# Windowed attention and an MLP mixer on one core: q and k of ten head pairs transposed by DMA instead of by TensorE

## The chip, the cores and the metric

One core of one Trainium2 chip runs the kernel. The metric is the device time of one execution, in microseconds. Three executions of the kernel before took 206.72, 207.12 and 207.36 us; the median is 207.12. A fourth execution ran under the hardware profiler, and every duration below is from it.

## What is computed

Attention with a window of 128 keys and 4 sink keys (batch 4, 8 heads, 768 positions, head size 64), and then a mixer on its output (model width 512): a small MLP over positions, added to its input, and an MLP over channels, added again. The inputs are float32; the kernel works in bf16 with float32 accumulation.

```python
scores = scale * np.matmul(q, k.transpose(0, 1, 3, 2))
is_sink = pos[None, :] < 4
rel = pos[:, None] - pos[None, :]
keep = is_sink | ((rel >= 0) & (rel < 128))
a = softmax(np.where(keep, scores, -1e9))
x = concat_heads(np.matmul(a, v))                        # 4 x 768 x 512
h = np.maximum(x.transpose(0, 2, 1) @ w_tok1, 0.0) @ w_tok2   # 768 -> 256 -> 768
u = x + h.transpose(0, 2, 1)
out = u + np.maximum(u @ w_ch1, 0.0) @ w_ch2             # 512 -> 1536 -> 512
```

## The kernel before

**The unit of attention is a pair of heads.** There are 16 pairs, p = 0 to 15, four for each batch element. A pair's q and k are held as bf16 tiles q_bf and k_bf, 128 partitions x (6 rows, 2 heads, 64 columns). Scores need the head dimension on the partitions, so both are transposed into qT and kT (128 x 768: 64 columns of each of the two heads by 768 positions). Scores are matmuls of kT and qT into PSUM, ACT takes the exponential into pT, DVE masks it, and matmuls of pT with v_aug (v with a column of ones) give values and sums, which DVE turns into x_sb.

**Loads.** Pairs 0 to 3 come as float32 over SP's queue. Pairs 4 to 15 are loaded and cast by POOL's queue, one DMA for each head of q and of k (96 KB in bf16, 'half' below; `load_cast`, line 104), one DMA for v (192 KB, `load_v`). Six pairs of q_bf and k_bf are kept (NQ, line 54); the load of pair p waits until pair p - 6 has been transposed (line 984). The weights, w_ch1 and w_ch2 in four quarters each, go through the same queue between the pairs (lines 1025 to 1040): w_ch2's quarters come behind pairs 4 to 7. In `rows_of` (line 85) a partition holds six consecutive rows of q, which lie together in HBM (1536 bytes).

**Transposing.** For pairs 5 to 15, `transposed` (line 447) gives PE 24 transposes of 64 rows (12 of q, 12 of k; line 455) into one of the two score banks in PSUM. ACT or DVE copy qT and kT out (lines 129 and 131), undoing the order of the rows, and DVE then clears a part of the bank (`cleared`, line 470). Pair 4 and the first four are transposed by `turn` (line 429) in other banks. qT has 2 buffers, kT has 4 (NKB).

**Order.** The program is written by a planner, class `Plan`, that holds a cost and dependences for each piece of work (`Op`) and a clock for each engine, and issues instructions in the order that these give; each engine then runs its own instructions in that fixed order. PE's work comes in three lists: the first batch element's attention; `main`, the channel MLP of all four (`mix_channels`: v1 units with w_ch1, out_part units with w_ch2); and `side`, the attention and token mixing of the other three (`attention_and_tokens`, line 846). How main and side are interleaved is a written list, MERGED: "9/25" puts side unit 9 once 25 main units have been placed. Work with 64 rows is grouped in bursts, since PE loses time in changing between 64 and 128 rows. The burst that scores pair p begins with the transposes of pair p + 1 (lines 855 to 863).

**The end of the work.** out_part sums twelve matmuls in a PSUM bank, DVE adds u (line 924) into one of three o_sb buffers, and SP issues the store (line 930).

Of the kernel before, what the change touches and what calls it, by code (L numbers as in the profile page):

```python
# [10 lines left out]
BF16 = mybir.dt.bfloat16  # L11
# [5 lines left out]
def kernel(  # L17
# [13 lines left out]
    nc = tc.nc  # L31
    B, H, S, D = q.shape
    P = 128
    NT = S // P
# [10 lines left out]


    MERGED = (
        "1/0 0/2 2/4 3/8 4/15 5/17 6/17 7/19 8/24 9/25 10/25 11/27 12/27 13/29 14/29 15/30 16/32 17/32 18/35 "
        "19/36 20/38 21/38 22/38 23/41 25/42 26/42 24/42 27/44 28/48 29/50 31/52 30/52 32/56 33/57 34/57 "
        "35/60 36/61 39/63 40/63 41/65 42/67 38/67 37/67 43/71 44/76 45/76 46/76 47/80 50/82 48/82 49/82 "  # L50
        "51/86 52/92 53/95 54/95 55/95 56/100 57/102 58/102 59/105 60/106 62/115 67/115 63/115 61/118 64/120 "
        "65/121 66/128 68/130 69/131 70/133 71/135 72/135 73/135 74/138"
    )
    NQ = 6
    NPT = 3
    MASKED_BY_PE = [(p, g) for p in range(NHP) for g in range(NT // 2) if (p, g) != (NHP - 1, 0)]

    singles = ctx.enter_context(tc.tile_pool(name="singles", bufs=1))
    qkv_pool = ctx.enter_context(tc.tile_pool(name="qkv", bufs=NQ))
    raw_pool = ctx.enter_context(tc.tile_pool(name="raw", bufs=4))  # L60
    att_pool = ctx.enter_context(tc.tile_pool(name="att", bufs=2))
    pt_pool = ctx.enter_context(tc.tile_pool(name="pt", bufs=NPT))
    mix_pool = ctx.enter_context(tc.tile_pool(name="mix", bufs=2))
    v1_pool = ctx.enter_context(tc.tile_pool(name="v1", bufs=1))
# [16 lines left out]
    in_order = tc.keep_in_program_order  # L81
# [3 lines left out]
    def rows_of(pidx, n):  # L85

        b, hp = pairs[pidx]
        return (q, k)[n][b, 2 * hp:2 * hp + 2].rearrange("h (p j) d -> p h j d", j=NT)

    def load_raw(pidx):  # L90
        raw = []
# [6 lines left out]
    bfs = {}  # L98
# [28 lines left out]
    def copy(e, out, in_):  # L127
        if e == "ACT":
            in_order(nc.scalar.activation(out, in_, AF.Copy))  # L129
        else:  # L130
            in_order({"DVE": nc.vector, "POOL": nc.gpsimd}[e].tensor_copy(out=out, in_=in_))  # L131
# [10 lines left out]
    done = {}  # L142
    tiles = {}
# [7 lines left out]
    def keep_warm(n, slot):  # L151
# [18 lines left out]
        out=ident, in_=ident, compare_op=ALU.not_equal, fill=1.0, base=0, pattern=[[-1, P]], channel_multiplier=1,  # L170
    ))
    in_order(nc.gpsimd.affine_select(
        out=mask_add[:, :, 0], in_=mask_add[:, :, 0], compare_op=ALU.is_ge,
# [3 lines left out]
        out=mask_add[:, :, 1], in_=mask_add[:, :, 1], compare_op=ALU.is_ge,  # L177
# [6 lines left out]
    NKB = 4  # L184
    kTb = [singles.tile([P, S], BF16, name=f"kT{n}") for n in range(NKB)]
# [8 lines left out]
    for n in range(4):  # L194
# [3 lines left out]
            out=v_sink_f[rows, odd::2, i, 0:D],  # L198
            in_=v[0].rearrange("(p o i) s d -> i o s p d", i=2, o=2)[i, odd, 0:n_sink],
# [186 lines left out]
    def piece(ns, fn, deps, need, then, keys=()):  # L386
        op = Op({}, fn, deps, then, size=float(ns))
        op.need, op.keys = need, keys
        return op

    QH = NT // 2

    def prepare(p):

        kT = kTb[p % NKB]
        parts = 2 if p <= NHP else 1

        def evict(e, n, part):
            name = ("q", "k")[n]
            if n:  # L400
                t = kT
            elif ("qT", p) in tiles:
                t = tiles["qT", p]
            else:
                t = tiles["qT", p] = att_pool.tile([P, S], BF16, name="qT2")
            to = t.rearrange("d (x p j) -> d x p j", x=2, j=NT)
            copy(e, to if parts == 1 else to[:, part], tiles["ps_" + name, p] if parts == 1 else tiles["ps_" + name, p][part])

        free = ([("sk", p - 2)] if p >= 2 else [], [(n, p - NKB) for n in ("s", "sk")] if p >= NKB else [])
        if parts == 2:  # L410
            cost = {"DVE": 540.0, "ACT": 500.0}
        else:
            cost = {"DVE": 950.0} if p < NHP else {"DVE": 950.0, "ACT": 900.0}
        for n, name in enumerate(("qT", "kT")):
            done[name, p] = [
                Op(dict(cost), lambda e, n=n, part=part: evict(e, n, part), free[n]) for part in range(parts)
            ]
            for part, op in enumerate(done[name, p]):
                op.urgent = (3 - part) * (p < NHP)
        tiles["kT", p] = kT  # L420
# [26 lines left out]
    def transposed(p):  # L447

        def run():
            ps = turned_bank(p)  # L450
            for n in range(2):
                for j in range(NT):
                    for x in range(2):
                        rows = ds(D * x, D)
                        in_order(nc.tensor.transpose(ps[:, x, n, j], bfs[p, n][rows, j], ident[rows, rows]))  # L455
                tiles["ps_" + "qk"[n], p] = ps[:, :, n].rearrange("d x j p -> d x p j")

        then = [*done["qT", p], *done["kT", p]]
        then.append(cleared(p, then))
        return piece(  # L460
            350, run, [done["q_bf", p], done["k_bf", p]], {"sc": [then]}, then, [("tq", p), ("tk", p)],
        )

    def turned_bank(key):

        tiles["ps_turned", key] = bank("sc")
        t = tiles["ps_turned", key].bitcast(BF16).rearrange("d x n b c -> d x n (b c)")[:, :, :, 2 * D:8 * D]
        return t.rearrange("d x n (j p) -> d x n j p", j=NT)

    def cleared(key, readers):  # L470

        op = Op(
            {"DVE": 400.0}, lambda e: in_order(nc.vector.memset(tiles["ps_turned", key][0:D, :, :, 3], 0.0)), readers,
        )
        op.urgent = 2
        return op

    def width(g):
        return 3 * P if g == NT // 2 - 1 else 4 * P
# [19 lines left out]
    def scores(p, g):  # L499
# [49 lines left out]
        x = done["exp", p, g] if by_pe else Op({}, None)  # L549
        x.cost, x.fn, x.deps = {"ACT": 190.0 + 1.5 * width(g)}, exp, [("pv", p - NPT)] if p >= NPT else []  # L550
        x.urgent = 2 * (p < NHP)
# [9 lines left out]
    def score_sinks(p):  # L561
# [17 lines left out]

        x = Op({"ACT": 580.0}, exp, [("pv", p - NPT)] if p >= NPT else [])  # L580
        for n in (p - 1, p):
# [94 lines left out]
    def sink_rows(p):  # L676
        def both(e):
            for i in range(2):
                r = D * i + ODD * (p % 2)
                copy(e, v_sinks[p % NHP][r:r + n_sink, i], vs[p][0:n_sink, i, 0])  # L680

        done["vs", p] = Op({"ACT": 440.0, "DVE": 400.0}, both, [done["v", p], done["pv", p - NHP]])
        return done["vs", p]
# [138 lines left out]
    def first_attention():  # L822
# [5 lines left out]
        for p in range(NHP):  # L828
            for g in range(NT // 2):
                if (p, g) in MASKED_BY_PE:  # L830
                    masks.append(masked(p, g))
# [14 lines left out]
    def attention_and_tokens():  # L846

        parts, units = [], []
        first, last = NHP, len(pairs) - 1
        prepare(first)  # L850
        units += [turn(first, n) for n in range(2)]
        for p in range(first, last + 1):
            b, hp = pairs[p]
            pieces = []
            if p < last:
                prepare(p + 1)
                pieces.append(transposed(p + 1))
            pieces.append(scores(p, 0))
            if p > first:
                pieces.append(sink_values(p - 1))  # L860
            if p == last:
                pieces.append(turned_u(b, 0, "sc"))
            units.append(burst(*pieces))
            if p > first:
                units += [values(p - 1, i) for i in range(2)]
            pieces = [scores(p, 1), scores(p, 2)]
            if hp == 0 and p > first:
                units.append(mix_h(b - 1, 1, 0, NTOK))
                units += [mix_u(b - 1, 1, st, 2) for st in range(0, NT, 2)]
                pieces.append(turned_u(b - 1, 1))  # L870
            if hp == NHP - 1 and p < last:
                pieces.append(turned_u(b, 0))
            if hp % 2 == 0:
                pieces.append(score_sinks(p + 1))
            units.append(burst(*pieces))
            units[-1].then.append(sink_rows(p))
            if hp == 2:
                units.append(mix_h(b, 0, 0, NTOK))
                units += [mix_u(b, 0, st, 2) for st in range(0, NT, 2)]
            if hp == 0 and p > first:  # L880
                parts.append(units)
                units = []
        units += [pv(p, half) for half in range(2)]
        units.append(mix_h(b, 1, 0, NTOK))
        units += [mix_u(b, 1, st, 2) for st in range(0, NT, 2)]
        units.append(burst(turned_u(b, 1)))
        return parts + [units]
# [108 lines left out]
    plan = Plan()  # L996
# [98 lines left out]
```

## Time and profile before

| | |
|---|---|
| median of three runs | 207.12 us |
| profiled execution | 206.41 us |
| its span, first to last instruction | 204.6 us |
| PE busy | 197.6 us, 97% |
| ACT, DVE busy | 113.8 us, 112.4 us |
| share of PE in the chain that ended last | 85% |
| DMA queue of POOL | 11.80 MB in 67,232 packets |
| DMA queue of SP | 9.45 MB in 5,968 packets |
| DMAs of q_bf, k_bf from issue to landing, median | 6.8 us, 5.9 us |

The span is the time from the first to the last instruction that the profiler recorded; 1.8 us of the execution lie around it. Engines are PE (TensorE matmuls), PEld (its weight loads), DVE, ACT, POOL and SP. A row of the order of time gives start, duration, engine, line, operation, the tile written and the tiles read, and how many instructions were put together. A matmul's end is modelled, so two that follow each other overlap in these rows. The instruction order of a program, with the semaphores that an instruction waits for, is known for both kernels from their builds; durations are known for the kernel before alone.

### The profile page before, as it was taken

The numbers are of one execution on the slowest core, as the hardware profiler recorded it, in microseconds if no ns is written. First come the engines' busy times: TensorE is split into PE (matmuls) and PEld (weight loads), VectorE is DVE, ScalarE is ACT, GpSimd is POOL, SyncE is SP. The second block draws the span as 40 slices with busy tenths as digits, with TensorE's granted clock in tenths as the row PEclk, the third lists the DMA queues.
The fourth block names the chain that finished last, engine by engine and source line by source line (L and its number), as shares of the span: only waits on it lengthen the run. The fifth ranks groups of instructions, "written<-read, shape, count | busy, mean of one in ns | idle before, by whom it ended". The sixth has DMA issues, their size and how long they took to land.

```text
span 204.6 us, 5496 instructions
## 1 busy us (share of the span) xinstructions
PE 197.6 (97%) x2377; PEld 119.3 (58%) x2377; DVE 112.4 (55%) x238; ACT 113.8 (56%) x195; POOL 67.3 (33%) x86
## 2 busy tenths in 40 slices
PE   6798999999999999999999999999999999999994
PEld 2345985566665665667656545666655645665453
DVE  4775653657788766866948557572654361001222
ACT  4898668879706535886563145886750114773000
POOL 6299859795699891450000000000000000000000
DMA  6999999999999999193001112100002112000223
GB/s 193 292 257 188 169 177 191 160 172 206 157 180 189 187 184 198 22 128 20 3 0 54 53 64 97 51 5 0 0 3 103 51 54 103 0 3 0 103 103 103
DMA packets 73223, 21.58 MB, mean 105 GB/s; under 512 B 63216, under 2 KB 70256, under 8 KB 73200
## 3 DMA queue, kind: packets, MB, share of 16 engines
q0 software_dynamic: 67232, 11.80, 73.1%
q1 hardware_dynamic: 5968, 9.45, 13.1%
q8 instruction: 18, 0.29, 0.6%
q14 instruction: 5, 0.04, 0.1%
HBM read 26.75 MB, written 6.29 MB: 161 GB/s over the span
## 4 chain that ended last, share of the span: by engine, by line
PE 85%; DMA 6%; DVE 3%; ACT 2%; POOL 1%; issue 1%; SPq 0%; POOLq 0%; ACTq 0%
PE ps_mx L122 77%; PE ps_sc L122 4%; DMA w_tok<-in_moe_w_tok_dram 4%; DMA v_sink_f<-in_v_dram 2%; PE ps_sc L455 2%; POOL v_aug L115 1%; DVE kT L131 1%; PE ps_mx L427 1%; ACT pT L539 1%; ACT qT L129 1%; PE ps_mx L125 1%; SPq L197 0%; ACT uT L129 0%; DVE u_sb L751 0%; DVE x_sb L650 0%
## 5 line engine op out<-in xcount | busy, mean ns | idle before, releaser
L122 PE MATMUL ps_mx<-uT,w_ch 128*128 128x384 bf16 x384 | 67.1, 326 | 0.1
L122 PE MATMUL ps_mx<-w_ch,v1T 128*128 128x512 bf16 (+2 forms) x312 | 66.9, 363 | 0.0
L539 ACT ACTIVATE pT<-ps_sc 128x1024 bf16<-128x1024 f32 (+1 forms) x48 | 44.4, 952 | 13.0 <-PE ps_sc L122 12.9
L122 PEld LDWEIGHTS <-w_ch 128*128 128x128 bf16 x384 | 36.0, 98 | 23.9 <-issue 1.2
L135 ACT ACTIVATE v1T<-ps_mx 128x384 bf16<-128x384 f32 x77 | 37.7, 490 | 19.5 <-PE ps_mx L122 18.9
L122 PEld LDWEIGHTS <-v1T 128*128 128x128 bf16 x312 | 28.3, 98 | 27.6 <-issue 0.5
L924 DVE TENSOR_TENSOR o_sb<-ps_mx,u_sb 128x512 f32<-128x512 f32 x23 | 15.8, 687 | 34.6 <-PE ps_mx L122 34.6
L122 PEld LDWEIGHTS <-w_tok 128*128 128x128 bf16 x192 | 18.3, 98 | 5.9 <-DMA w_tok<-in_moe_w_tok_dram 0.7
L107 POOL DMA_DIRECT2D q_bf<-in_q_dram x24 | 19.6, 822 | 4.4 <-DMA w_ch<-in_moe_w_ch_dram 2.2
L107 POOL DMA_DIRECT2D k_bf<-in_k_dram x24 | 19.6, 820 | 4.1 <-DMA w_ch<-in_moe_w_ch_dram 1.7
L751 DVE TENSOR_TENSOR u_sb<-ps_mx,x_sb 128x512 bf16<-128x512 f32 x20 | 13.2, 687 | 13.0 <-PE ps_mx L122 12.9
L115 POOL DMA_DIRECT2D v_aug<-in_v_dram x16 | 16.4, 1026 | 8.3 <-ACT v_sink L129 7.1
L131 DVE COPY kT<-ps_sc 128x768 bf16<-128x768 bf16 x11 | 10.5, 958 | 13.4 <-ACT qT L129 13.4
L122 PEld LDWEIGHTS <-pT 128*128 128x128 bf16 x352 | 14.1, 98 | 3.3 <-issue 0.6
L129 ACT ACTIVATE qT<-ps_sc 128x768 bf16<-128x768 bf16 x11 | 8.9, 810 | 12.3 <-PE ps_sc L455 12.1
L122 PE MATMUL ps_mx<-v_aug,pT 128*128 128x65 bf16 x352 | 15.6, 194 | 0.0
L547 DVE TENSOR_TENSOR pT<-pT,mask_main 128x1024 bf16<-128x1024 bf16 (+1 forms) x24 | 14.3, 619 | 1.3 <-ACT pT L539 1.3
L122 PE MATMUL ps_sc<-qT,kT 64*64 64x192 bf16 (+3 forms) x288 | 14.4, 248 | 0.0
L135 ACT ACTIVATE h1T<-ps_mx 128x512 bf16<-128x512 f32 (+1 forms) x8 | 4.1, 517 | 17.1 <-PE ps_mx L122 16.9
L122 PE MATMUL ps_mx<-h1T,w_tok 128*128 128x256 bf16 x96 | 13.2, 273 | 0.0
L137 DVE TENSOR_SCALAR v1T<-ps_mx 128x384 bf16<-128x384 f32 x19 | 10.4, 549 | 4.9 <-PE ps_mx L122 4.9
L122 PE MATMUL ps_mx<-x_sb,w_tok 128*128 128x256 bf16 x96 | 12.0, 273 | 0.5 <-DMA w_tok<-in_moe_w_tok_dram 0.4
(68 smaller groups left out, 156.6 us busy)
## 6 DMA issues: line engine op xcount, KB each, us to landing
out_dram<-o_sb SPq DMA_DIRECT2D x23, 256.0 KB, 2.0
v_aug<-in_v_dram POOLq DMA_DIRECT2D x16, 192.0 KB, 7.2
w_ch<-in_moe_w_ch_dram POOLq DMA_DIRECT2D x8, 384.0 KB, 8.8
q_bf<-in_q_dram POOLq DMA_DIRECT2D x24, 96.0 KB, 6.8
k_bf<-in_k_dram POOLq DMA_DIRECT2D x24, 96.0 KB, 5.9
q_f<-in_q_dram SPq DMA_DIRECT2D x4, 384.0 KB, 5.0
k_f<-in_k_dram SPq DMA_DIRECT2D x4, 384.0 KB, 5.7
w_tok<-in_moe_w_tok_dram POOLq DMA_DIRECT2D x2, 384.0 KB, 7.7
```

The lines of the kernel that those rows point to most:

```text
L107: in_order(nc.gpsimd.dma_start(out=out[:, h], in_=rows[:, h]))
L115: in_order(nc.gpsimd.dma_start(out=v_aug.rearrange("p i t d -> p (i t) d")[:, :, 0:D], in_=v[b].rearrange("h s d -> (h s) d")[2 * hp * S:2 ...
L122: in_order(nc.tensor.matmul(*args, skip_group_check=True, **kwargs))
L129: in_order(nc.scalar.activation(out, in_, AF.Copy))
L131: in_order({"DVE": nc.vector, "POOL": nc.gpsimd}[e].tensor_copy(out=out, in_=in_))
L135: in_order(nc.scalar.activation(out, in_, AF.Relu))
L137: in_order(nc.vector.tensor_scalar_max(out=out, in0=in_, scalar1=0.0))
L455: in_order(nc.tensor.transpose(ps[:, x, n, j], bfs[p, n][rows, j], ident[rows, rows]))
L539: in_order(nc.scalar.activation(part(tiles["pT", p][:, :, ds(2 * g, 2)]), of_keys(tiles["ps_s", p, g])[:, :, 0:width(g)], AF.Exp, scale=scale,
L547: in_order(nc.vector.tensor_tensor(out=pt, in0=pt, in1=m, op=ALU.mult))
L751: in_order(nc.vector.tensor_tensor(out=u_part(b, g, s0, n), in0=tiles["ps_u", b, g, s0], in1=x_sb[b][:, s0:s0 + n, c0:c0 + cn], op=ALU.add,))
L924: in_order(nc.vector.tensor_tensor(out=o_sb.rearrange("p (g c) -> p g c", g=2), in1=u_rows(b, st), in0=tiles["ps_out", b, st].rearrange("p ...
```

## The change

From pair 6 on (BY_DMA), q_bf and k_bf are loaded with row p of each of the six 128-row tiles on partition p, and `prepare` no longer makes transposes and copies. It plans two operations on SP instead, a DMA each, which read the bf16 tile in SBUF and write qT or kT in SBUF transposed. They wait for the loads and for the buffers that they write (4 of qT now, 4 of kT). The burst of pair p no longer holds the transposes of pair p + 1 when p + 1 is 6 or more; the score bank, the copies and the clearing that belonged to them are gone. A load of pair p + 6 now waits for pair p's transfers. MERGED is another list. The output stores share SP's queue with the transfers. The planner's costs for a transfer are 1700 ns on SP and 2500 ns until it has landed.

```diff
     MERGED = (
-        "1/0 0/2 2/4 3/8 4/15 5/17 6/17 7/19 8/24 9/25 10/25 11/27 12/27 13/29 14/29 15/30 16/32 17/32 18/35 "
...
+        "1/0 0/2 2/4 3/8 4/16 5/16 6/17 7/17 8/21 9/23 10/25 11/25 12/27 13/29 15/29 14/30 16/32 17/32 18/32 "
...
     NPT = 3
+    BY_DMA = 6
...
-    att_pool = ctx.enter_context(tc.tile_pool(name="att", bufs=2))
+    att_pool = ctx.enter_context(tc.tile_pool(name="att", bufs=4))
...
-        return (q, k)[n][b, 2 * hp:2 * hp + 2].rearrange("h (p j) d -> p h j d", j=NT)
+        return (q, k)[n][b, 2 * hp:2 * hp + 2].rearrange(
+            "h (j p) d -> p h j d" if pidx >= BY_DMA else "h (p j) d -> p h j d", j=NT,
+        )
...
+    def turned_by_dma(p):
+
+        free = ([("sk", p - 4)], [(n, p - NKB) for n in ("s", "sk")])
+
+        def transfer(n):
+            if n:
+                t = tiles["kT", p] = kTb[p % NKB]
+            else:
+                t = tiles["qT", p] = att_pool.tile([P, S], BF16, name="qT2")
+            in_order(nc.sync.dma_start(
+                out=t.rearrange("c (j p) -> c j p", j=NT), in_=bfs[p, n].rearrange("p j h d -> p (j h d)"), transpose=True,
+            ))
+
+        for n, name in enumerate("qk"):
+            op = Op({"SP": 1700.0}, lambda e, n=n: transfer(n), [done[name + "_bf", p], *free[n]], lag=2500.0)
+            done[name + "T", p] = [op]
+            done["t" + name, p] = op
+            plan.pending.append(op)
+
     def prepare(p):
+        if p >= BY_DMA:
+            return turned_by_dma(p)
...
                 prepare(p + 1)
-                pieces.append(transposed(p + 1))
+                if p + 1 < BY_DMA:
+                    pieces.append(transposed(p + 1))
```

## The prediction

> **What bounds the kernel now.** I read the page's busy times first, then the busy table by stage, then the order of time inside one burst, then the DMA issues.
>
> ```profile
> span 204.6 us, 5496 instructions
> ...
> PE 197.6 (97%) x2377; PEld 119.3 (58%) x2377; DVE 112.4 (55%) x238; ACT 113.8 (56%) x195; POOL 67.3 (33%) x86
> ...
> DMA  6999999999999999193001112100002112000223
> ```
>
> PE has 97% of the span, DVE and ACT half of it. The DMA row (40 slices of 5.1 us) is full until 82 us and almost empty afterwards.
>
> ```profile
> core 0: us, PE busy (x) PEld busy (x) DVE busy (x) ACT busy (x) POOL busy (x), PEclk, DMA share, GB/s
> 30.00:40.00 10.00, 10.00 (x123) 5.71 (x122) 5.81 (x12) 8.19 (x16) 7.87 (x10) 1.00 1.99 174
> 40.00:50.00 10.00, 10.00 (x124) 6.31 (x123) 6.20 (x14) 8.36 (x16) 8.47 (x11) 1.00 1.68 185
> 50.00:60.00 10.00, 10.00 (x128) 6.25 (x126) 7.56 (x15) 5.04 (x9) 7.45 (x10) 1.00 2.22 162
> 60.00:70.00 10.00, 10.00 (x209) 6.05 (x208) 7.65 (x18) 6.39 (x9) 10.00 (x13) 1.00 2.15 198
> ```
>
> PE is busy for all of 30 to 70 us at a granted clock of 1.00, and the later rows say the same up to 200 us, but for 0.15 us. So the time is PE's list of work, and an edit is worth what it takes from that list, less the waits it adds. The DMA share stands near 2: the engines are shared by overlapping packets, and in this stretch a new transfer has no idle engine to go to.
>
> ```profile
> 86.33 0.33 PE L122 MATMUL ps_mx<-uT,w_ch 128*128 128x384 bf16 x1
> ...
> 86.59 0.35 PE L455 MATMUL ps_sc<-ident,q_bf 64*128 64x64 bf16 x12
> ...
> 86.78 0.34 PE L455 MATMUL ps_sc<-ident,k_bf 64*128 64x64 bf16 x12
> ...
> 86.95 0.38 PE L122 MATMUL ps_sc<-qT,kT 64*128 64x256 bf16 x4
> ```
>
> This is one burst. A matmul's row ends late because it is pipelined, so its price is the distance from its start to the next start. The 24 transposes begin at 86.59 and the scores at 86.95: **0.36 us a pair** (the chain of waits books 0.46, the last one's tail included). The changeover from 128 to 64 rows, about 0.1 us ahead of 86.59, belongs to the burst, which stays.
>
> **The change, part by part.**
>
> 1. Gone from PE: the transposes of ten pairs, 10 x 0.36 = **3.6 us**, all on the bounding engine. The two programs' instruction order agrees: 2377 matmuls become 2137, which is 10 x 24 fewer, and the 74 changes between 64-row and 128-row work stay 74.
>
> 2. Gone from ACT and DVE: per pair a copy of qT (810 ns, L129), of kT (958 ns, L131) and a clearing (272 ns, L473). Both engines have idle time (5.87 and 6.17 of 10 us in 100 to 110), so most is worth nothing. Twice PE waits for what a copy delays: at 70.56 for x_sb (L650), which DVE begins only after kT's copy of 68.39 to 69.35, and at 98.75 for an eviction behind kT's copy and the clearing. Against the usual distance of such matmuls I read 0.21 and 0.23 us lost there. I take **0.4 us**; nothing is the other bound.
>
> 3. Added on SP: 20 transfers of 192 KB. The trace has no transposing transfer. Nearest rows:
>
> ```profile
> out_dram<-o_sb SPq DMA_DIRECT2D x23, 256.0 KB, 2.0
> v_aug<-in_v_dram POOLq DMA_DIRECT2D x16, 192.0 KB, 7.2
> ```
>
> A 256 KB store from SP lands in 2.0 us, and in 4.0 to 5.1 us while loads run (its largest values, at 76 and 80 us). I take 5 us for the second transfer of a pair to land after its issue, and 1.7 us between the two issues, the planner's own number in the diff (a store's issue on SP takes 0.33). For the burst it must land in time. I laid the changed program's PE order out with the distances that before shows, and set each pair's first wait against the landing of its second k half in before. Pair 6: needed at 47.9, landed 40.05. Pair 7: 52.2 and 43.9. Pair 8: 63.8 and 55.3. Pair 9: 74.8 and 59.1. Pair 10: 84.7 and 64.0; later pairs have 19 us or more. With q issued when it lands (38.7 for pair 6), k 1.7 behind or when it lands, and 5 us, pair 6 is ready at 45.4: 2.5 us to spare, and pairs 7 and 8 have 3 us. So the latency is covered by the lead of one pair that the new order leaves; past 2.5 us more, each microsecond is paid once (a late pair pushes all behind it back too). Stores wait behind the transfers on SP: the first one behind pair 8's k, which landed at 55.3 against a store at 57.86, and three o_sb buffers stand behind that. I cost this at nothing.
>
> 4. Added on the 16 DMA engines, where I see the real price. Loads of POOL's queue land one behind another: q and k halves 0.63 us apart, v 1.51 us apart. A transfer in between holds up all loads behind it. The first four (pairs 6 and 7) run between 39 and 49 us, with the last quarters of w_ch2 queued behind them.
>
> ```profile
> 40.65 3.01 POOL L140 DMA_DIRECT2D w_ch<-in_moe_w_ch_dram  x4
> ...
> w_ch<-in_moe_w_ch_dram POOLq DMA_DIRECT2D x1, 384.0 KB, 8.7
> ```
>
> The third quarter is issued at 42.14 and takes 8.67 us: it lands at 50.81. In the changed order PE asks for it at 53.06 (53.28 before). **Cover: 2.25 us**; the fourth has 2.4. Price of a transfer: a store moves its 256 KB in about 0.7 us (two stores at 153 to 157 us make 0.52 MB in two short peaks near 390 GB/s), so 192 KB take **0.53 us**; four make 2.1. The upper bound is a v load, of the same 192 KB in 1536 small packets: 1.51. Nothing speaks for a gain; the lower bound is 0, if transfers inside SBUF fit between packets that wait for HBM. I take the store, the only row of SP's queue.
>
> 5. The loads of pairs 6 to 15 keep 768 packets of 128 B a half, but a partition's six rows no longer lie together in HBM. v's loads have that layout, and cost 1.51 / 1536 x 768 = 0.755 for as many packets against 0.63: 0.12 us more a half, eight halves ahead of w_ch2: **1.0 us**. Bounds 0 and 1.0; I take 1.0.
>
> Parts 4 and 5 make the third quarter late by 2.1 + 1.0 - 2.25 = **0.8 us** (0 to 4.8), and PE waits for it once. Past that the queue is later still, but pairs 9 to 15 have 15 us or more.
>
> 6. The merge: the same work with as many changeovers. What it moves is priced by the waits it meets, and in before PE's waits of all kinds past 30 us, changeovers aside, come to about 1 us. I cost it at 0, with 1 us either way.
>
> Sum: 206.41 (profiled execution; its span is 204.6 and 1.8 lies around it) - 3.6 - 0.4 + 0.8 = **203.2**. The median, 207.12, stands 0.7 above that execution, so I forecast **203.9**; its own range is 203.0 to 205.5.
>
> The Trainium skill has two figures for part 4 that contradict each other. "DMA: Bandwidth & Descriptors", section "Latency and other measured facts", gives 261 GB/s for a DMA transpose; an estimate from it is 0.75 us a transfer, and the sum of 203.2 would be 204.2. "VectorE: DVE Perf Modes", section "The three transpose paths", gives 1309 ns for a 128x128 transpose by DMA against 390 ns on TensorE, and advises TensorE where PSUM will do; six blocks in a row would be 7.9 us. No run here shows either yet; the 0.36 us for a whole pair of q and k on PE is far below its 390 ns a block, so I don't carry that table's DMA figure into the sum.
>
> **The rivals.**
>
> A. *Nothing is late.* Transfers between SBUF rows slip between load packets and the new layout is free: 206.41 - 4.0 = 202.4, or 203.1 by the median. For it: the store does overlap with loads. Against it: landings do spread by about 0.7 us for each store between 58 and 75 us.
>
> B. *The transposing transfer costs the engines as much as a v load*, because it is cut small. One place, the third quarter of w_ch2: 4 x 1.51 + 1.0 - 2.25 = 4.8 us late, so 206.41 - 4.0 + 4.8 = 207.2, by the median 207.9, slower than before. It decides from (4.0 + 2.25 - 1.0) / 4 = 1.3 us a transfer. For it: every small-packet row here (128 B) costs at least 1.26 us for 192 KB. Against it: SBUF to SBUF needs no HBM. At 2.5 us a transfer it is near 212.
>
> C. *SP's queue does one transfer after another, each as long as a v load takes to land* (7.2 us). A pair then takes 14.4 us against PE's pace of (132.9 - 47.9) / 9 = 9.4, and PE waits for each: 38.7 + 10 x 14.4 + 68 us of work behind pair 15's wait = 251. It decides from 4.7 us a transfer. Against it: stores issued 2.6 us apart (153.81 and 156.40) land in 2.0 each, and planner costs that can be compared lie at their rows (950 for kT's copy of 958). The second page's rule, by its figure, would be of this kind: an estimate of 264 us.
>
> D. *The written merge loses what the transposes gave*, by 2 to 3.5 us of small waits: 205.5 to 207.5. Against it: the 74 equal changeovers.
>
> That the change doesn't do what it says is excluded by the instruction order: 240 transposes gone, 20 transfers there.
>
> **How the numbers follow.** Forecast 0.42, A 0.20, B 0.22, C 0.10, D 0.06. A measurement of this kernel tells 0.3% (0.6 us) from no change. Faster: forecast, A and a third of D, 0.64. Same (206.5 to 207.7): a quarter of B and half of D, 0.08. Slower: the rest of B and D, and C, 0.28. The range holds the forecast, A, D and rather more than half of B, 0.8 together: 202.7 to 209.0; C stays outside.
>
> **What would show it.** Right: no L455 row past pair 5; the PE row of w_ch,v1T near 53 us waiting under 1.5 us for w_ch; q and k halves about 0.75 us apart; transfers landing 3 to 5 us after issue. Wrong: PE waits on a transfer at the scores of pairs 6 to 8 (latency), w_ch2 later than 54 us (B), or a wait at every pair (C).

## The result, and the profile after

The kernel after takes **212.88 us**, the median of four runs (210.87 to 214.24), against 207.03 for four runs of the kernel before (206.72 to 207.36): a ratio of 1.025 [1.020, 1.030]. It is slower, where 203.9 was forecast and 209.0 was the upper end of the range. The profiled execution, 214.24, counts as a slow one, over 1.5% above the fastest of its four, and the ratio leaves it out, but its mean clock of 0.984 is like that of the other three (0.982 to 0.984). Its span of 212.5 stands against 204.6, and the 7.9 between the two spans are looked for below.

The page of the kernel after, from its busy times, its slices and its DMA queues:

```profile
span 212.5 us, 5003 instructions
...
PE 194.7 (92%) x2117; PEld 117.5 (55%) x2137; DVE 101.5 (48%) x218; ACT 107.8 (51%) x185; POOL 67.9 (32%) x86
...
PEclk9999999999967999999999999999999999999999
DMA  6999999999999999999999511200001212000222
...
q1 hardware_dynamic: 21968, 13.38, 29.7%
```

PE works 2.9 us less than before, DVE 10.9 and ACT 6.0 less, so the work did go; PE now stands still for 17.8 us of the span instead of 7.0. Two slices, from 58 to 69 us, have a granted clock of 0.6 and 0.7, which before has nowhere. The DMA row is full until 117 us instead of 82. SP's queue has 21,968 packets instead of 5,968: 16,000 for 20 transfers, 800 each (768 of 256 bytes and 32 of 4, by the trace's packet records).

The busy table by stage of after, the stretches that the prediction showed of before:

```profile
core 0: us, PE busy (x) PEld busy (x) DVE busy (x) ACT busy (x) POOL busy (x), PEclk, DMA share, GB/s
30.00:40.00 10.00, 9.83 (x125) 5.57 (x123) 5.81 (x12) 8.22 (x16) 6.79 (x9) 1.00 1.98 174
40.00:50.00 10.00, 8.95 (x95) 5.43 (x92) 5.83 (x12) 8.04 (x16) 7.44 (x10) 1.00 2.02 136
50.00:60.00 10.00, 4.57 (x66) 2.96 (x67) 4.08 (x10) 3.73 (x5) 3.49 (x4) 0.99 1.29 177
60.00:70.00 10.00, 8.26 (x38) 4.47 (x40) 1.72 (x3) 1.20 (x2) 8.04 (x10) 0.66 2.22 154
```

Past 22 us PE stands still for 9.6 us in all (0.3 before), and 8.2 of them lie between 40 and 70 us. The order of time says why; first SP, then PE, with the idle time ahead of an instruction and what ended it in brackets:

```profile
40.17 1.32 SPq L405 DMA_TRANSPOSE qT<-q_bf  x1
41.67 1.89 SPq L405 DMA_TRANSPOSE kT<-k_bf  x1
44.13 1.62 SPq L405 DMA_TRANSPOSE qT<-q_bf  x1
46.33 4.87 SPq L405 DMA_TRANSPOSE kT<-k_bf  x1
```

```profile
51.38 0.39 PE L125 MATMUL ps_sc<-qT,kT 64*128 64x256 bf16 x4 [2.43 <-DMA kT<-k_bf]
...
61.69 0.61 PE L125 MATMUL ps_mx<-qT,kT 64*32 64x512 bf16 x2 [5.68 <-DMA kT<-k_bf]
62.23 2.74 PE L125 MATMUL ps_mx<-w_ch,v1T 128*128 128x512 bf16 x6
```

Pair 6's kT is issued at 41.67 and lets PE go at 51.4: 9.7 us. Pair 7's is issued at 46.33, SP itself is held by it for 4.87 us, and PE gets on at 61.7: 15.3 us. By the packet records the four transfers pass one after another, in 3.5, 4.5, 5.6 and 5.2 us, so pair 7's kT stands in line until 55.9. The chain that ended last goes through that one transfer:

```profile
46.33 15.31 DMA kT<-k_bf
```

After the second wait the matmuls of w_ch and v1T are 427 ns apart until 64.8, where at the full clock they are 216 apart, and those of x_sb 213 instead of 109. The table by stage has the clock in its third column from the right, 1.00 being full:

```profile
61.69:66.00 4.31, 4.31 (x14) 1.91 (x15) 0.00 (x0) 0.60 (x1) 4.04 (x5) 0.50 2.42 155
67.00:70.00 3.00, 2.95 (x20) 1.82 (x20) 1.72 (x3) 0.60 (x1) 3.00 (x5) 1.00 1.93 161
```

The clock is 0.50 from 59.9 to 66.7 us. Six matmuls of the first kind (5 x 0.21 + 0.19) and nine of the second (9 x 0.10) come to 2.2 us. The balance of the span: - 3.6 (transposes) + 2.4 + 5.7 (the two waits) + 2.2 (half clock) = 6.7. Of the 1.2 that are left, 0.9 lie at the start: PE's first matmul that reads x_sb begins at 19.84 instead of 18.95. No step touches that stage, and the thirteen other traces of this case, which share it, have 18.95 to 20.57. The last 0.3, and some 1.1 us of small waits past 70 us that the balance doesn't hold, stay unexplained.

The Trainium skill, "TensorE: Matmul & The Clock Gate", section "What's actually happening", says that TensorE falls to half clock after an idle window of some 3.4 us and comes back after as much busy time. The trace agrees: the wait of 2.4 us at 49 cost no clock; that of 5.7 was followed by 0.50, and 5 us of work later the clock was 1.00 again. Run 8 below fits less well: no wait there is longer than 2.4 us, and the clock is 0.50 for 3.4 us all the same.

The DMA issues of after, from issue to landing, and the third quarter of w_ch2 alone:

```profile
qT<-q_bf SPq DMA_TRANSPOSE x10, 8.0
kT<-k_bf SPq DMA_TRANSPOSE x10, 7.9
```

```profile
w_ch<-in_moe_w_ch_dram POOLq DMA_DIRECT2D x1, 384.0 KB, 15.0
```

A transfer takes 8 us, not 5, and that quarter lands at 58.44 instead of 50.81. PE had no wait for it, since it stood before pair 7's scores until 61.7: two consequences of one contention, of which only the longer is paid.

### The profile page after: what moved, and what is told of

Its sections match the earlier page's. It is cut to its first block, busy times and chain, and to the rows that moved or that the text cites. A ratio compares the mean times of both kernels' runs of the same rounds, so it can differ in the third digit from the quotient of the medians.

```text
span 212.5 us, 5003 instructions
## 1 busy us (share of the span) xinstructions
PE 194.7 (92%) x2117; PEld 117.5 (55%) x2137; DVE 101.5 (48%) x218; ACT 107.8 (51%) x185; POOL 67.9 (32%) x86
## 3 DMA queue, kind: packets, MB, share of 16 engines
q1 hardware_dynamic: 21968, 13.38, 29.7%
## 4 chain that ended last, share of the span: by engine, by line
PE 81%; DMA 10%; POOL 3%; DVE 1%; issue 1%; ACT 1%; SPq 0%; POOLq 0%
PE ps_mx L125 75%; DMA kT<-k_bf 7%; PE ps_sc L125 5%; DMA v_sink_f<-in_v_dram 3%; POOL v_aug L118 2%; PE ps_mx L451 1%; POOL w_tok L143 1%; ACT pT L563 1%; PE ps_mx L128 1%; SPq L200 0%; PE ps_mx L463 0%; POOL k_bf L134 0%; POOL q_bf L134 0%; DVE u_sb L775 0%; POOL v_sink L134 0%
## 5 line engine op out<-in xcount | busy, mean ns | idle before, releaser
L125 PE MATMUL ps_mx<-w_ch,v1T 128*128 128x512 bf16 (+2 forms) x295 | 66.2, 367 | 1.2 <-issue 0.5
L138 ACT ACTIVATE v1T<-ps_mx 128x384 bf16<-128x384 f32 x80 | 39.3, 491 | 16.5 <-PE ps_mx L125 15.5
L125 PEld LDWEIGHTS <-v1T 128*128 128x128 bf16 x312 | 28.8, 98 | 28.6 <-issue 2.0
L125 PEld LDWEIGHTS <-w_tok 128*128 128x128 bf16 x192 | 19.2, 101 | 6.6 <-issue 0.5
L125 PEld LDWEIGHTS <-kT 64*64 64x64 bf16 (+2 forms) x320 | 7.6, 101 | 17.3 <-DMA kT<-k_bf 8.8
L138 ACT ACTIVATE h1T<-ps_mx 128x512 bf16<-128x512 f32 (+1 forms) x9 | 4.7, 526 | 23.5 <-PE ps_mx L125 23.4
L140 DVE TENSOR_SCALAR v1T<-ps_mx 128x384 bf16<-128x384 f32 x16 | 8.8, 554 | 13.5 <-PE ps_mx L125 13.3
L125 PE MATMUL ps_mx<-h1T,w_tok 128*128 128x256 bf16 x96 | 13.7, 273 | 0.0
L125 PE MATMUL ps_mx<-x_sb,w_tok 128*128 128x256 bf16 x96 | 12.9, 287 | 0.2 <-DMA w_tok<-in_moe_w_tok_dram 0.2
L674 DVE TENSOR_TENSOR x_sb<-ps_mx,recip 128x384 bf16<-128x384 f32 x22 | 12.0, 554 | 0.5
```

Source lines behind the costliest of these rows:

```text
L125: in_order(nc.tensor.matmul(*args, skip_group_check=True, **kwargs))
L138: in_order(nc.scalar.activation(out, in_, AF.Relu))
L140: in_order(nc.vector.tensor_scalar_max(out=out, in0=in_, scalar1=0.0))
L674: in_order(nc.vector.tensor_tensor(out=x_sb[b][:, :, ds((2 * hp + i) * D, D)], in0=tiles["ps_o", p, i][:, :, 0:D], in1=tiles["recip", p, i ...
```

## The experiments

The theory after the first look (**contention**): the transfers of pairs 6 and 7 run beside w_ch2's quarters, each slows the other, and pairs 8 to 15 are harmless. Rivals: the **layout** slows the loads, the **merge** makes the waits, the transfer is **slow in itself**, or the price of a transfer is its **bytes** and not its packets. There are four sets, each on one chip with its own runs of before: runs 1, 2, 3 and 4 (before: median 206.89); both of 5, 6 and the first of 7 (206.75); 3b, the second of 7 and 8 (206.80); and 9 (207.16).

**1. Transfers from pair 8 on, the rest as after.**

```diff
-    BY_DMA = 6
+    BY_DMA = 8
```

> The changed kernel with transfers from pair 8 on only; pairs 6 and 7 are transposed by PE again. Theory 1 (the four transfers of pairs 6 and 7 meet w_ch2's quarters and each other, and PE waits for them and for nothing later): PE loses 2 x 0.36 us of the gain and gets the two waits of 2.6 and 5.9 us back, so about 203.5 to 204.5 us. Theory 2 (every pair's transfer is late, the rest is only hidden behind the first wait): the wait moves to pair 8, 207 to 212. Theory 3 (the written merge loses the time): 210 or more, as the changed kernel.

Measured: 204.08 us (203.97 to 204.78), ratio 0.987 [0.984, 0.989].

```profile
span 202.2 us, 5090 instructions
...
PE 194.1 (96%) x2165; PEld 118.0 (58%) x2185; DVE 103.0 (51%) x220; ACT 109.3 (54%) x189; POOL 67.5 (33%) x86
```

Two pairs less turn a loss of 2.5% into a gain of 1.3%. The 2.8 us that are gained fit the 8 x 0.36 = 2.9 of the transposes. The sixteen transfers land in 7.5 and 7.7 us (medians), hardly sooner than in the kernel after, and nobody waits for them: what decides is where they fall, not their number. The first is issued at 55.56, when w_ch2's last quarter has landed (54.24).

**2. The kernel before with transfers that nobody reads.** PE still transposes; from pair 6 on, SP also issues the two transposing transfers of the pair into tiles that are never read.

```diff
     def prepare(p):
+        if p >= 6:
+            def transfer(n):
+                t = att_pool.tile([P, S], BF16, name="unread", bufs=4)
+                in_order(nc.sync.dma_start(
+                    out=t.rearrange("c (j p) -> c j p", j=NT), in_=bfs[p, n].rearrange("p j h d -> p (j h d)"), transpose=True,
+                ))
+            for n, name in enumerate("qk"):
+                plan.pending.append(Op({"SP": 1700.0}, lambda e, n=n: transfer(n), [done[name + "_bf", p]], lag=2500.0))
```

> The kernel before, with the 20 transfers added into tiles that nobody reads: PE transposes all pairs as before. It measures what the transfers cost the other DMAs and nothing else. If they slow the loads (1.4 us for each of the first four, read from w_ch2's landings in the changed kernel), w_ch2's third quarter lands 3 to 5 us after PE asks for it and the time is 209 to 212. If the whole loss is PE waiting for the transfers themselves, 206.5 to 207.5.

Measured: 215.33 us (212.59 to 218.92), ratio 1.040 [1.036, 1.044], with no new layout, no new merge and no reader. It is more than the 209 to 212 that I had expected; the fastest execution, 212.59, which is the profiled one, is 5.7 us above the median of before. The waits of PE from 29 to 90 us (what it waited for: us in total, times, longest):

```profile
PE ps_mx L122 <- DMA w_ch<-in_moe_w_ch_dram: 2.7, 2, 1.7
PE ps_mx L122 <- DVE o_sb L934: 2.1, 1, 2.1
```

The third quarter of w_ch2 takes 14.23 us from issue to landing, against 8.67. Shared among the four transfers of pairs 6 and 7: 5.56 / 4 = **1.39 us of the load queue for each**. (Half of the fourth is still to come when that quarter lands; by the fourth quarter, which lands when all four have passed, it is (15.94 - 9.86) / 4 = 1.52.) So transfers that nobody reads make a kernel slower than before. The second wait is for an o_sb buffer: its store is issued at 78.60, right behind a transfer on SP, and lands in 7.23 us, where the stores of before at 76 and 80 us took 4.0 to 5.1.

**3. The layout alone.** The kernel before, with the loads of pairs 6 to 15 in the scattered-row layout, and the copies out of PSUM changed to suit.

```diff
-        return (q, k)[n][b, 2 * hp:2 * hp + 2].rearrange("h (p j) d -> p h j d", j=NT)
+        return (q, k)[n][b, 2 * hp:2 * hp + 2].rearrange(
+            "h (j p) d -> p h j d" if pidx >= BY_ROWS else "h (p j) d -> p h j d", j=NT,
+        )
...
+            if p >= BY_ROWS:
+                to = t.rearrange("d (j x p) -> d x p j", x=2, j=NT)
```

> The kernel before with the new load layout of pairs 6 to 15 (row p of each 128-row tile on partition p) and PE's transposes copied out accordingly; no transfers. The recorded prediction prices the layout at 0.12 us a half, under the cover of 2.25 us: 206.5 to 207.5. If the scattered rows are what made the loads late: 209 or more, and q and k halves landing over 0.75 us apart.

Measured: 277.62 us, ratio 1.341 [1.338, 1.344]. This experiment upset its own question; the group of copies (busy us, mean ns of one, then idle time):

```profile
L134 DVE COPY kT<-ps_sc 128x768 bf16<-128x768 bf16 x11 | 36.7, 3337 | 45.4 <-ACT qT L132 45.4
```

Pair 5's copy, in the old layout, is among the eleven; the other ten, which step through PSUM and through SBUF, took 3575 ns on DVE instead of 958, and 3588 on ACT instead of 810. The halves of q and k still landed 0.63 us apart. Mended in **3b**, with the elements in the order of their addresses on both sides:

```diff
+            if p >= BY_ROWS:
+                return copy(
+                    e, t.rearrange("d (j x p) -> d x j p", x=2, j=NT), tiles["ps_" + name, p].rearrange("d x p j -> d x j p"),
+                )
```

> The kernel before with the load layout of the changed kernel for pairs 6 to 15 and PE's transposes, as e3_layout, but copied out along the 64 positions that lie together on both sides. e3_layout showed the halves 0.63 us apart, so the layout is free for the loads; what made it slow was its copies of 3.3 us, strided on both sides. Now 206.3 to 207.3; if the scattered rows cost something after all, over 207.5.

Measured: 206.16 us (205.46 to 207.17), ratio 0.9965 [0.994, 0.999]; the halves land 0.63 to 0.66 apart and the third quarter takes 8.71 us. **The layout costs nothing that can be measured.** The rival falls.

```profile
L134 DVE COPY kT<-ps_sc 128x768 bf16<-128x768 bf16 x11 | 6.5, 594 | 13.4 <-ACT qT L132 13.4
```

Without pair 5's, kT's copy takes 558 ns instead of 958; the 0.6 us of the total may be that. ACT's copy of qT takes 811 as before.

**4. The merge alone.** The kernel before with the list of after.

```diff
     MERGED = (
-        "1/0 0/2 2/4 3/8 4/15 5/17 6/17 7/19 8/24 9/25 10/25 11/27 12/27 13/29 14/29 15/30 16/32 17/32 18/35 "
+        "1/0 0/2 2/4 3/8 4/16 5/16 6/17 7/17 8/21 9/23 10/25 11/25 12/27 13/29 15/29 14/30 16/32 17/32 18/32 "
...
```

> The kernel before with the changed kernel's written merge alone. Theories 1 and 2: 206.5 to 208 (the order is worth little by itself). Theory 3: 210 or more.

Measured: 212.5 us (212.14 to 212.97), ratio 1.027 [1.024, 1.029], outside what I had expected. PE waits 2.9 us in four places for DVE's clearing of a score bank (line 473) between 29 and 150 us, and 1.5 us for ACT's pT and for x_sb beside that. Bursts without transposes need no such bank, so the list may suit them better. Taken for itself it would explain the whole loss, so the next run had to part the two.

**5. Transfers from pair 8 on, with the list of before.**

```diff
     MERGED = (
-        "1/0 0/2 2/4 3/8 4/16 5/16 6/17 7/17 8/21 9/23 10/25 11/25 12/27 13/29 15/29 14/30 16/32 17/32 18/32 "
+        "1/0 0/2 2/4 3/8 4/15 5/17 6/17 7/19 8/24 9/25 10/25 11/27 12/27 13/29 14/29 15/30 16/32 17/32 18/35 "
...
-    BY_DMA = 6
+    BY_DMA = 8
```

> As e1_from8 (transfers from pair 8 on) with the written merge of the kernel before. If the new merge is fitted to the transfers and worth something with them, slower than e1_from8 by 0.5 to 2 us: 204.5 to 206. If the merge is worth nothing either way: 204.

Measured: 203.69 us (203.44 to 204.35), ratio 0.985 [0.982, 0.988], against 204.08 and 0.987 with the new list, in another set. Where the transposes are gone, the list is worth nothing that can be told, and it makes none of the waits of run 4. A third list, entries 4 to 12 of the old one and the rest new:

```diff
-        "1/0 0/2 2/4 3/8 4/16 5/16 6/17 7/17 8/21 9/23 10/25 11/25 12/27 13/29 15/29 14/30 16/32 17/32 18/32 "
+        "1/0 0/2 2/4 3/8 4/15 5/17 6/17 7/19 8/24 9/25 10/25 11/27 12/27 13/29 15/29 14/30 16/32 17/32 18/32 "
...
-    BY_DMA = 6
+    BY_DMA = 8
```

> As e1_from8, with the nine entries of the merge that place side units 4 to 12 taken from the kernel before. e1_from8 shows one PE wait of 0.7 us at 45.5 us, for the clearing of the score bank of a transposed pair, where the new merge puts a burst sooner than the old one. If that wait goes, 203.2 to 203.8; if another takes its place, 204 as e1_from8.

Measured: 203.73 us (202.04 to 204.73), ratio 0.982 [0.977, 0.987]. A wait of 0.5 us of PE at 45.7 that run 1 has is gone, but the three lists can't be told apart in time.

**6. Is the transfer slow in itself?** The kernel before, and the transfers of pairs 10 to 15 issued behind pair 15's scores, when no load runs.

```diff
+        if p == len(pairs) - 1:
+            def transfer(m, n):
+                t = att_pool.tile([P, S], BF16, name="unread", bufs=4)
...
+            for m in range(p - 5, p + 1):
+                for n in range(2):
+                    plan.pending.append(Op({"SP": 1700.0}, lambda e, m=m, n=n: transfer(m, n), [("s", p)], lag=2500.0))
```

> The kernel before with 12 unread transposing transfers (pairs 10 to 15) after pair 15's scores, when the loads are done. It measures a transfer without company. Theory 1 (packet for packet with the loads): landing about 3 us after issue and 768 packets in 1.0 to 1.3 us. If a transposing transfer is slow by itself: 7 us or more, as the median of 8.0 in the changed kernel. Time near before's, 206.5 to 208, since PE waits for none of it.

Measured: 207.22 us, ratio 1.001 [0.998, 1.003]. Issue to landing, and two issues on SP:

```profile
unread<-q_bf SPq DMA_TRANSPOSE x6, 2.8
unread<-k_bf SPq DMA_TRANSPOSE x6, 2.8
```

```profile
132.46 1.23 SPq L398 DMA_TRANSPOSE unread<-k_bf  x1
133.79 1.23 SPq L398 DMA_TRANSPOSE unread<-q_bf  x1
```

By itself a transfer lands in 2.8 us, and the next one follows 1.35 us behind. It is slow only beside loads.

**7. Bytes or packets?** Run 2 again with plain copies in place of the transposing ones: the same 192 KB in 128 pieces of 1536 bytes.

```diff
+                t = att_pool.tile([P, S], BF16, name="unread", bufs=4)
+                in_order(nc.sync.dma_start(out=t, in_=bfs[p, n].rearrange("p j h d -> p (j h d)")))
```

> The kernel before with 20 unread transfers in the same places as in e2_unread, of the same 192 KB from SBUF to SBUF, but plain copies with a partition's 1536 bytes in one piece. If the price of a transfer goes by its packets (768 of 256 bytes when transposed, 128 when plain), w_ch2's third quarter lands under 1 us later than in before instead of 5.6 us, and the time is 206.7 to 208. If it goes by bytes or by what reading and writing SBUF takes, the time is near e2_unread's, over 211.

Measured: 208.0 us (207.65 to 208.14), ratio 1.0055 [1.004, 1.007].

```profile
unread<-q_bf SPq DMA_DIRECT2D x10, 192.0 KB, 5.8
unread<-k_bf SPq DMA_DIRECT2D x10, 192.0 KB, 6.1
```

The third quarter takes 11.37 us, 2.70 more than before, where I had expected less than 1: 0.67 a copy. Then the same plain copy cut into 768 pieces of 256 bytes by a gap in the tile that it writes:

```diff
+                t = att_pool.tile([P, NT, P + 16], BF16, name="unread", bufs=4)
+                in_order(nc.sync.dma_start(out=t[:, :, 0:P], in_=bfs[p, n].rearrange("p j h d -> p j (h d)")))
```

> As e5_plain, plain copies that nobody reads, but written into rows with a gap, so that each copy is cut into 768 packets of 256 bytes as a transposing transfer is. If the packets alone make the price, w_ch2's third quarter takes 14 us from issue to landing as in e2_unread (11.4 in e5_plain, 8.7 without transfers), about 1.4 us a copy, copies land in about 8 us, and the time is 210 to 216. If transposing itself costs the engines something, the quarter lands clearly sooner than 14 us, and the time is between e5_plain and e2_unread.

Measured: 210.1 us (209.89 to 211.64), ratio 1.019 [1.013, 1.025].

```profile
unread<-q_bf SPq DMA_DIRECT2D x10, 192.0 KB, 7.7
```

```profile
w_ch<-in_moe_w_ch_dram POOLq DMA_DIRECT2D x1, 384.0 KB, 13.1
```

4.4 us later, 1.10 a copy. So the load queue loses 0.67 us to 192 KB in large pieces, 0.43 more to small ones, and 0.29 more where they are transposed (1.39 of run 2). **Packets make more of the price than transposing does.** These are single traces. Without a transfer the third quarter took 8.67 to 9.30 us in eight of them and 10.73 in run 4's, so the 1.15 us between 14.23 and 13.08 are near the scatter. By the fourth quarter the three prices are 0.59, 1.24 and 1.52, in the same order.

**8. Where the edge is.** Run 5 with the transfers from pair 7 on.

```diff
-    BY_DMA = 6
+    BY_DMA = 7
```

> As e7_merge_before, with transfers from pair 7 on. Two transfers instead of four beside w_ch2's quarters: at 1.39 us each the third quarter is 2.8 us later, against a cover of 2.2 to 2.5, and pair 7's k, issued near 44.5, must land by 53.5. So the edge: a PE wait of 0.3 to 2 us against 0.36 gained, 203.5 to 205.5. If the loss of the changed kernel were proportional to the number of early transfers, half of it: 207 or more.

Measured: 209.22 us (208.26 to 209.88), ratio 1.012 [1.007, 1.017]; I had expected a gain. The waits of PE from 29 to 90 us:

```profile
PE ps_mx L125 <- DMA kT<-k_bf: 2.4, 1, 2.4
PE ps_mx L125 <- DMA w_ch<-in_moe_w_ch_dram: 1.4, 2, 1.2
```

Pair 7's two transfers alone make the third quarter 3.2 us late (11.89), and pair 7's own kT, issued at 46.07, lets PE go at 59.2. Three waits, of 0.2, 1.2 and 2.4 us, lie between 53 and 59.2, and the clock falls behind them:

```profile
60.51:63.93 3.42, 3.42 (x13) 1.51 (x11) 1.84 (x3) 0.00 (x0) 3.42 (x5) 0.50 2.28 155
```

The edge is between pair 7 and pair 8, where w_ch2's quarters end.

**9. A version that beats both?** Run 5, and the contiguous copies of 3b for pairs 5 to 7, which PE still transposes.

```diff
     BY_DMA = 8
+    BY_ROWS = 5
...
-            "h (j p) d -> p h j d" if pidx >= BY_DMA else "h (p j) d -> p h j d", j=NT,
+            "h (j p) d -> p h j d" if pidx >= BY_ROWS else "h (p j) d -> p h j d", j=NT,
```

> As e7_merge_before (transfers from pair 8 on, merge of the kernel before), with pairs 5 to 7 loaded in the layout of rows too, so that PE's transposes of these three pairs are copied out along positions that lie together (DVE's kT copy took 594 instead of 958 ns in e3b_layout). Gain over before: 8 x 0.36 = 2.9 us from PE's list, and up to 0.4 from DVE's shorter copies: 203.0 to 203.9. If the copies are covered, as DVE's idle time says, equal to e7_merge_before: 203.7.

Measured: 204.63 us (203.67 to 205.1), ratio 0.986 [0.983, 0.990], as run 5 alone: the shorter copies gain nothing that shows. The best version is the change from pair 8 on, 1.3 to 1.8% faster than before by runs 1, 5 and 9 and the third list.

**What the two queues do to each other.** The trace's packet records of after, counted over 52 to 58 us, have 798 packets of 1024 bytes (w_ch2's) and 795 of 256 bytes (the transfers'): the queues go forward packet for packet. With the packets of 4 bytes the view counts 830 and 827 (q0 is POOL's queue, q1 SP's):

```profile
q0 software_dynamic: 830, 0.82, 88.6%
q1 hardware_dynamic: 827, 0.20, 36.3%
```

Each advances at some 133 packets a microsecond there, so the transfers of pair 7 take 5.6 and 5.2 us for 768 packets, where in the quiet of run 6 one takes 1.09, about 700 a microsecond. Beside q, k and v, whose packets have 128 bytes, the queues also go one for one, but three times as fast; here is the microsecond from 83 to 84:

```profile
q1 hardware_dynamic: 416, 0.11, 80.0%
q0 software_dynamic: 417, 0.05, 79.7%
```

This fits the later transfers' doing less harm: past pair 7 each passes in 1.2 to 3.0 us. Pair 6's kT and both transfers of pair 7 stood in line when w_ch2 began to run at 47, and the last of them took 15 us. No run moves w_ch2 itself away from the transfers, so its part is read from these counts and from where the edge lies.

The Trainium skill, "DMA: Bandwidth & Descriptors", section "Queues, rings and completion order", says that each DMA engine takes turns between its queues at packet granularity. The trace agrees with that, by the 798 and 795 packets.

## Why the prediction was wrong

**Step 1, the transposes: right.** 3.6 us for ten pairs; eight pairs gave 2.8 in run 1.

**Step 2, copies and clearing: 0.4 us, not to be told apart.** Run 9 shows no gain from shorter copies where PE turns only pairs 5 to 7; the 0.6 us of run 3b may be a part of it. The 5.87 and 6.17 us that the step calls idle time are busy times of ACT and DVE; idle are 4.13 and 3.83, which changes nothing.

**Step 3, the latency: this is where the prediction failed.** I took 5 us from a store's largest values, which come from packets of 2048 bytes at 76 and 80 us, when w_ch2 has long passed, and said that it is covered up to 2.5 us more. Measured: 8 us in the middle and 9.7 and 15.3 for the two that PE met. "Past 2.5 us more, each microsecond is paid once" was the right rule with too small an input, and two of the pairs paid: 2.4 + 5.7 us. What the 5 us had no room for is the line: the four transfers follow each other, and each takes turns with w_ch2's packets. Half the clock after the longer wait, 2.2 us, was priced nowhere. Stores behind transfers cost nothing in after, as forecast, but 2.1 us in run 2.

**Step 4, the price to the load queue: mis-sized.** I took 0.53 from a store's bytes, and kept a v load's 1.51 for the range. Run 2 measured 1.39. The kernel after itself has (15.00 - 8.67) / 4 = 1.58. The upper bound was the nearer row; like the transfer (768 packets of 256 bytes) a v load is cut small (1536 of 128). By its bytes alone a transfer would cost 0.67 (run 7), near the forecast. I had the third quarter land 3.1 us later than before (2.1 + 1.0); it landed 7.6 later, 1.3 of them through a later issue.

**Step 5, the layout: 1.0 us expected, none found** (run 3b). Reading v's extra 0.25 us a load as the price of scattered rows was wrong.

**Step 6, the merge: 0, right as far as tried** (run 5 against run 1, both with transfers from pair 8 on; the change itself was not run with the old list), though the same list costs the kernel before 5.6 us (run 4): its price hangs on the rest of the program, and 1 us either way was no bound for it.

**The rivals.** A is excluded by the two waits and by run 2. B had the mechanism and the side of the result, and its 1.51 is near 1.39; its 207.9 fell short since it looked at the load queue alone. A transfer that holds up loads is held up by them as well, and the readers of qT and kT came ahead of w_ch2's. C had the queue right, one transfer after another: the first four pass in 4.7 us each on the mean, which is its limit. It fails past pair 7, where they pass in 1.2 to 3.0 and no pair waits. D didn't decide: run 5 has the old list and gains as much. The sign that the text named for latency, a wait at the scores of pairs 6 to 8, is what the trace shows; so is B's, w_ch2 later than 54 us (58.44), but PE paid nothing for it.

What stays open: the 0.9 us at the start of the profiled execution, which I put down to variation without a run that isolates it; why w_ch2's third quarter took 10.73 us in run 4, which has no transfers; and why pair 7's kT held SP for 4.87 us, which fits a full line of packets but was not tried by itself.

## What to carry to other kernels

Before moving work to the DMA queues, look at what else is in flight at that moment, and count packets, not bytes: a transfer in 768 small packets beside a load in large ones goes at the load's packet rate, and makes the load late too, and transfers on one queue stand in line behind each other. A price from a quiet stretch, or from a median over the kernel, says nothing of the two transfers that meet the busiest one; start the change where the large loads have passed, and it may pay. A wait of PE can have a second price, the clock after it.

## What the runs showed of the hardware that was not expected

- The same transfer (128 x 768 bf16, SBUF to SBUF, transposing) lands in 2.8 us alone, in 6.7 to 8.7 beside the other loads of the kernel after, and needed 15.3 from issue to its reader's start behind three others beside loads with 1024-byte packets.
- Two queues share the engines packet for packet: 798 of 1024 bytes to 795 of 256 over 6 us, and 409 of 128 bytes to 416 of 256 in the microsecond from 83 to 84; each queue goes at 133 packets a microsecond in the first case and at some 412 in the second.
- A copy of 128 x 768 bf16 from PSUM to SBUF took 3575 ns on DVE and 3588 on ACT with strides on both sides, 958 and 810 with a stride on one, and 558 and 811 in runs of 64 elements.
- Rows of 256 bytes in the float32 source, far apart or six of them together: some 0.63 us a half either way.
- The clock was halved for 6.8 us behind a wait of 5.7 us, and in run 8 for 3.4 us behind three waits of which the longest was 2.4 us.
